# Weight sums behind the transforms: twelve of eighteen sums move to the end of the transform stage, in buffers of the next stage

## The chip, the cores and the metric

The kernel runs on one core of a Trainium2 chip. The core has five engines with an instruction stream each: PE (TensorE, matmuls), DVE (VectorE), ACT (ScalarE), POOL (GpSimd) and SP (SyncE, which only issues DMAs here). An engine takes its instructions one after the other; an instruction can carry waits on semaphores that others raise. The metric is the device time of one execution in microseconds (us), as a median over runs. Lower is better.

## The reference

Eight sequences of 3008 positions and 256 channels go through a real FFT over the positions, a complex 256x256 mix with a soft threshold, and the inverse FFT. Each of the 24064 resulting rows then goes through a gated feed-forward layer with 1536 features.

```python
X = np.fft.rfft(x, axis=1)
Yr = Xr @ w_r - Xi @ w_i + b_r
Yi = Xr @ w_i + Xi @ w_r + b_i
Yr = np.sign(Yr) * np.maximum(np.abs(Yr) - lam, 0.0)   # Yi likewise
y = np.fft.irfft(Y, n=x.shape[1], axis=1)
...
gate = 1.0 / (1.0 + np.exp(-(x @ w_gate)))
val = x @ w_val
return (gate * val @ w_out).astype(np.float32)
```

## The kernel before

**Two halves.** In the first half the transforms are interleaved with a plain feed-forward over the first 9 chunks of 512 rows (`NPL = 9`). Each chunk has 12 feature blocks (`NF = 12`), so there are 108 units, numbered j (chunk c = j // 12, block f = j % 12). A unit is `ffn1` (12 matmuls into the PSUM banks pg and pv, a sigmoid on ACT at L583, a product on DVE at L585, a rounding hh on ACT at L593 and its rest hl on DVE at L594) and `ffn2` (6 matmuls into po, two units later). Between the units stand the steps of the transforms, and after the last forward step the inverse steps `inv_a` of the last two sequences: each takes a tile vf that SP loads (L501), multiplies it on PE (pia, L524), is copied out by ACT (yf, L535) and stored by SP to a DRAM tensor yd (L536). `load_v` is one step ahead of `inv_a`, and there are two vf tiles. In the second half the other rows go through the layer in pairs of chunks, in a form of a Winograd product with 7 instead of 8 block products. That needs sums of weight blocks (`make_t` for the first layer, into the DRAM tensor td; `make_s` for the second, into sd) and sums of input blocks (`first_operands` for the first pair).

**The weight sums.** They are POOL work alone. A `make_t` is 10 arithmetic instructions and a store (L706 to L716); a `make_s` is 13 and two stores (L726 to L742). The feature blocks form six pairs, so there are 12 `make_t` (two for each pair of blocks) and 6 `make_s`. The list `sums` holds them in this order, and the loop over the units takes one every third unit from j = 34 on, so the last comes at j = 85. Their tiles are tb and sa (ring `st`), tt (ring `ry`) and tr, sw and sr (ring `big`) of the transforms' pool p2 and of p3.

**The second half's buffers.** When the forward transforms are done (after j = 88 at the latest) the pool p2 is closed and p4 opened on the same memory. p4 holds nine tiles xop0 to xop8 for rounded operands (each a rounded half and a rest), four tiles w1s0 to w1s3 for first-layer weights, and a tile ypair. The helper `xop` hands out the nine in turn. Three go to `spare`; then the operands of the first pair take, in the order of `first_operands`, a11 xop3, s2 xop4, a12 xop5, s1 xop6, s3 xop7, a22 xop8.

```python
def xop(name):
    count[0] += 1
    return p4.tile([P, 2, HW], F32R, tag=f"xop{(count[0] - 1) % NCB}", bufs=1, name=name)
```

`first_operands` makes the first pair's operands in the last chunk: POOL forms s1 = a21 + a22 (L778, into s1f), s2 = s1 - a11 (L779, into s2f), s3 (L783, in ypair) and s4 (L787); for each operand ACT casts the rounded half (L774) and DVE subtracts the rest (L775). SP loads w1s0 to w1s2 for it (L757), and, placed by the planner of the second half into the same queue, one load of second-layer sums (w2s, L1342), the second pair's rows (ypair, L1198) and the fourth weight tile (w1s3, L1187).

**What sets the order.** In this part of the program a scheduler orders each engine's instructions when the kernel is built; the row order on each engine is then fixed. From the second half's first product on, the kernel's own planner (`arrange`) sets it.

Of the kernel before, what the change touches and what calls it, by code (L numbers as in the profile page):

```python
# [9 lines left out]
F32 = mybir.dt.float32  # L10
F32R = mybir.dt.float32r
# [19 lines left out]
NF2K, NR2K, NLD, NST, NBIG, NMF, NME, NVF, NVO, NHH, NSG, NYF, NYT = 5, 4, 3, 3, 5, 3, 2, 2, 1, 3, 2, 3, 3  # L31
# [10 lines left out]
EARLY = 4  # L42
AT_FIRST = 3
NCONV = 7


def _r12(v):
# [193 lines left out]
def tile_fft_mix_ffn(ctx: ExitStack, tc, x, w_r, w_i, b_r, b_i, w_one, w_out, mf, mi, mis, fa, ft, out):  # L241
    nc = tc.nc

    B, D, S = x.shape[0], w_r.shape[0], R1 * R2
    P = 128
    XR = x.shape[2]
    CT = D // P
    NF = w_one.shape[0]
# [54 lines left out]
    def big(name):  # L303
        return p2.tile([P, 4, D], F32, tag="big", bufs=NBIG, name=name)
# [238 lines left out]
    def result(name):  # L543
        return p3.tile([P, CW], F32, tag="ry", bufs=NYF, name=name)
# [152 lines left out]

    def make_t(fp, i):  # L700
        f0, f1 = 2 * fp, 2 * fp + 1
        g = nc.gpsimd
        b = p2.tile([P, 2, D], F32, tag="st", bufs=NST, name="tb").rearrange("p a (b n) -> p a b n", b=2)
        t = result("tt").rearrange("p (a b n) -> p a b n", a=2, b=2)
        for k, f in enumerate((f0, f1)):
            g.tensor_add(b[:, k], w1h[:, f, i], w1l[:, f, i])  # L706
        t = t.rearrange("p a b n -> p (a b) n")
        g.tensor_sub(t[:, 0], b[:, 1, 0], b[:, 0, 0])
        g.tensor_sub(t[:, 2], b[:, 1, 1], b[:, 1, 0])
        g.tensor_add(t[:, 1], t[:, 2], b[:, 0, 0])  # L710
        g.tensor_sub(t[:, 3], b[:, 0, 1], t[:, 1])
        r = p2.tile([P, 4, 2, P], F32R, tag="big", bufs=NBIG, name="tr")
        for k in (0, 2):
            g.tensor_copy(r[:, k:k + 2, 0], t[:, k:k + 2])
            g.tensor_sub(r[:, k:k + 2, 1], t[:, k:k + 2], r[:, k:k + 2, 0])
        g.dma_start(td[fp, i][:, 3:], r.bitcast(F32))  # L716
        for v, w in enumerate((w1h, w1l)):
            g.dma_start(td[fp, i][:, 0:2, v], w[:, f0, i].bitcast(F32))
            g.dma_start(td[fp, i][:, 2, v], w[:, f1, i, 1].bitcast(F32))

    def make_s(fp):
        g = nc.gpsimd
        if fp >= NH - FG:
            g.dma_start(pd[fp - NH + FG], w2[:, 2 * fp:2 * fp + 2].bitcast(F32))
        a = p2.tile([P, 2, D], F32, tag="st", bufs=NST, name="sa")
        g.tensor_add(a, w2[:, 2 * fp:2 * fp + 2, 0], w2[:, 2 * fp:2 * fp + 2, 1])  # L726
        a11, a21, a12, a22 = a[:, 0, :P], a[:, 0, P:], a[:, 1, :P], a[:, 1, P:]
        w = big("sw").rearrange("p a n -> p (a n)").rearrange("p (k n) -> p k n", n=P)
        zero = w[:, 7]
        g.memset(zero, 0.0)  # L730
        g.tensor_copy(w[:, 0], a11)
        g.tensor_sub(w[:, 1], zero, a12)
        g.tensor_sub(w[:, 3], zero, a22)
        g.tensor_add(w[:, 4], a22, a21)
        g.tensor_sub(w[:, 5], w[:, 4], a11)
        g.tensor_sub(w[:, 6], a11, a21)
        g.tensor_sub(w[:, 2], a12, w[:, 5])
        for k0, k1 in ((0, 4), (4, 7)):
            r = p2.tile([P, 4, 2, P], F32R, tag="big", bufs=NBIG, name="sr")[:, :k1 - k0]
            g.tensor_copy(r[:, :, 0], w[:, k0:k1])  # L740
            g.tensor_sub(r[:, :, 1], w[:, k0:k1], r[:, :, 0])
            g.dma_start(sd[fp // FG, k0:k1, :, fp % FG].rearrange("k p v n -> p k v n"), r.bitcast(F32))  # L742
# [307 lines left out]
    for j in range(NF, len(ffn)):  # L1050
        c, f = divmod(j, NF)
        ffn[j]()
        acc += rates[j >= part]
        if sums and j > 3 * NF - 3 and j % 3 == 1:
            sums.pop(0)()
        while side and (acc >= side[0][0] or j >= (part if len(side) > n_last else end) - 1):
            if len(side) == n_last and j < part:
# [435 lines left out]
```

## Time and profile before

| | us |
|---|---|
| median of 3 runs (lowest to highest) | 2704.79 (2703.63 to 2707.28) |
| the profiled execution | 2710.75 |
| its span, first to last instruction | 2708.9 |
| PE busy | 2662.7 |
| DVE busy | 2140.7 |
| ACT busy | 1670.5 |
| POOL busy | 1055.0 |

The profiled execution is one run of its own, 6.0 us above the median. Busy times are of that execution. A PE instruction's end is modelled, so a busy PE is not PE at its peak.

### The profile page before, as it was taken

The numbers are of one execution on the slowest core, as the hardware profiler recorded it, in microseconds if no ns is written. First come the engines' busy times: TensorE is split into PE (matmuls) and PEld (weight loads), VectorE is DVE, ScalarE is ACT, GpSimd is POOL, SyncE is SP. The second block draws the span as 40 slices with busy tenths as digits, with TensorE's granted clock in tenths as the row PEclk, the third lists the DMA queues.
The fourth block names the chain that finished last, engine by engine and source line by source line (L and its number), as shares of the span: only waits on it lengthen the run. The fifth ranks groups of instructions, "written<-read, shape, count | busy, mean of one in ns | idle before, by whom it ended". The sixth has DMA issues, their size and how long they took to land.

```text
span 2708.9 us, 45080 instructions
## 1 busy us (share of the span) xinstructions
PE 2662.7 (98%) x16763; PEld 2178.5 (80%) x16763; DVE 2140.7 (79%) x3100; ACT 1670.5 (62%) x2852; POOL 1055.0 (39%) x963
## 2 busy tenths in 40 slices
PE   9999999999999999999999999999999999999999
PEld 6778888888888878878788788878788788887877
DVE  5778888687789537888888888888888788888876
ACT  4565554545444446676677766766667667776665
POOL 1441012132235013544555445444554455544532
PEclk9999999999999999999999999999999999999999
DMA  9987655677666675878877888787877788787874
GB/s 294 293 285 197 193 151 168 204 208 208 179 185 179 171 218 164 251 237 251 263 238 246 251 246 265 236 247 237 256 249 242 234 269 239 244 259 243 259 227 135
DMA packets 257659, 617.82 MB, mean 228 GB/s; under 512 B 26464, under 2 KB 130656, under 8 KB 257440
## 3 DMA queue, kind: packets, MB, share of 16 engines
q1 hardware_dynamic: 222720, 521.29, 58.5%
q0 software_dynamic: 34608, 93.60, 16.2%
q8 instruction: 133, 2.18, 0.3%
q14 instruction: 86, 0.70, 0.1%
q10 hardware_dynamic: 112, 0.04, 0.0%
HBM read 440.50 MB, written 116.13 MB: 205 GB/s over the span
## 4 chain that ended last, share of the span: by engine, by line
PE 62%; DMA 14%; DVE 10%; ACT 6%; POOL 4%; issue 3%; SPq 0%; DVEq 0%; POOLq 0%; ACTq 0%
PE z L1155 15%; PE l2z L1155 13%; DMA h<-h 11%; PE c L1155 7%; PE pm L447 4%; PE b L1155 3%; PE pb L413 2%; POOL t L1320 2%; PE pia L524 2%; PE pg L577 2%; ACT op L1331 1%; PE pg L578 1%; POOL h L1320 1%; PE po L605 1%; PE pv L577 1%
## 5 line engine op out<-in xcount | busy, mean ns | idle before, releaser
L1155 PE MATMUL z<-xop,w1s 128*128 128x512 f32 x2592 | 684.3, 391 | 11.4 <-ACT tmp L1246 11.1
L1155 PE MATMUL l2z<-op,w2s 128*128 128x512 f32 x2331 | 599.8, 392 | 3.9 <-DMA w2s<-sd 1.9
L1155 PEld LDWEIGHTS z<-xop,w1s 128*128 128x128 f32 x2592 | 484.9, 188 | 123.8 <-ACT tmp L1246 24.0
L1155 PEld LDWEIGHTS l2z<-op,w2s 128*128 128x128 f32 x2331 | 436.2, 188 | 108.2 <-ACT tmp L1351 7.4
L1246 ACT COPY tmp<-z 128x512 f32<-128x512 f32 x684 | 394.3, 584 | 183.1 <-PE z L1155 175.2
L1333 DVE TENSOR_TENSOR op<-h,op 128x1024 fp32r<-128x1024 f32 (+1 forms) x444 | 472.2, 1078 | 24.9 <-ACT op L1331 19.5
L1331 ACT CAST op<-h 128x1024 fp32r<-128x1024 f32 (+1 forms) x444 | 366.4, 837 | 176.1 <-DMA h<-h 100.1
L1155 PE MATMUL c<-xop,w1s 128*128 128x512 f32 x1296 | 362.1, 392 | 5.1 <-DVE h L1287 3.3
L1293 POOL TENSOR_TENSOR h<-tmp 128x512 f32<-128x512 f32 x114 | 180.1, 1580 | 379.6 <-DVE tmp L1249 362.6
L1155 PEld LDWEIGHTS c<-xop,w1s 128*128 128x128 f32 x1296 | 242.7, 188 | 62.8 <-DVE h L1287 10.5
L1249 DVE TENSOR_TENSOR tmp<-tmp,c 128x512 f32<-128x512 f32 x342 | 231.5, 681 | 62.9 <-ACT tmp L1246 41.2
L1320 POOL TENSOR_TENSOR t<-h 128x512 f32<-128x512 f32 x111 | 173.3, 1562 | 158.0 <-DVE h L1285 158.0
L1265 ACT ACTIVATE tmp<-tmp 128x512 f32<-128x512 f32 x342 | 210.3, 632 | 28.4 <-DVE tmp L1249 28.4
L1314 POOL DMA_DIRECT2D h<-h x148 | 128.3, 900 | 165.8 <-DVE h L1289 56.0
L447 PE MATMUL pm<-w_sb,xsh 128*128 128x256 f32 x1008 | 184.4, 285 | 0.0
L1155 PE MATMUL b<-xop,w1s 128*128 128x512 f32 x648 | 182.3, 390 | 0.0
L447 PEld LDWEIGHTS pm<-w_sb,xsh 128*128 128x128 f32 x1008 | 152.9, 189 | 1.0 <-ACT xsh L429 0.4
L1320 POOL TENSOR_TENSOR h<-h 128x512 f32<-128x512 f32 x111 | 148.9, 1341 | 8.7
L458 ACT CAST yh<-yc 128x512 fp32r<-128x512 f32 x84 | 52.2, 621 | 147.0 <-DVE yc L437 146.9
L1155 PEld LDWEIGHTS b<-xop,w1s 128*128 128x128 f32 x648 | 121.3, 188 | 26.0 <-DVE tmp L1249 0.5
L447 PE MATMUL pm<-w_sb,xsl 128*128 128x256 f32 x504 | 139.6, 277 | 0.0
L585 DVE TENSOR_TENSOR sg<-sg,pv 128x512 f32<-128x512 f32 x108 | 74.1, 686 | 74.2 <-PE pv L579 56.0
(199 smaller groups left out, 4933.0 us busy)
## 6 DMA issues: line engine op xcount, KB each, us to landing
w1s<-td SPq DMA_DIRECT2D x228, 896.0 KB, 6.3
w2s<-sd SPq DMA_DIRECT2D x259, 384.0 KB, 4.3
h<-h POOLq DMA_DIRECT2D x74, 512.0 KB, 6.2
zf<-zd SPq DMA_DIRECT2D x96, 256.0 KB, 3.5
vf<-vd SPq DMA_DIRECT2D x128, 192.0 KB, 4.0
vd<-vz SPq DMA_DIRECT2D x84, 256.0 KB, 2.7
ypair<-yd SPq DMA_DIRECT2D x19, 1024.0 KB, 7.4
out_dram<-acc SPq DMA_DIRECT2D x76, 256.0 KB, 4.3
```

The source lines that it names most:

```text
L447: nc.tensor.matmul(o, l, r, start=(i == 0), stop=(i == len(mms) - 1))
L577: nc.tensor.matmul(t, wh, yth[:, ct], start=(ct == 0), stop=False)
L585: nc.vector.tensor_mul(h, sg, pv)
L1155: nc.tensor.matmul(o, ws[i], vs[j], start=first and not i and not j, stop=i == 1, skip_group_check=not first)
L1246: return t, on("ACT", 0.59, at, lambda: a_.copy(t.get(), z.get()), [z], [t], deps)
L1249: return on("DVE", 0.67, at, lambda: add(t.get(), s.get(), o.get()), [x for x in (s, o) if x is not t], [t], deps)
L1265: return on("ACT", 0.635, at, lambda: a_.activation(t.get(), (o or t).get(), AF.Sigmoid), [o] if o else [], [t], deps)
L1293: made[3, q] = on("POOL", 1.3, 16, lambda: g_.tensor_mul(at_h(3), g22.get(), v.get()), [g22, v], [h], [d22, e22], True)
L1314: return [[on("POOL", 0.9, at + q0, lambda q0=q0, q1=q1: g_.dma_start(h.get()[:, dst, q0:q1], h.get()[:, src, q0:q1], accum_op=ALU.add), [ ...
L1320: return [[on("POOL", 1.3, at + q, lambda q=q: g_.tensor_sub(v()[:, q], h.get()[:, a, q], h.get()[:, b, q]), [h], [o], sum((d[q] for d in ...
L1331: hi = on("ACT", 0.19 + 0.43 * n, at - 8 + q0, lambda q0=q0, q1=q1: a_.copy(t.get()[:, 0, q0:q1], v()[:, q0:q1]), [t_in], [t], sum((d[i] f ...
L1333: lo.append([on("DVE", 0.13 + 0.555 * n, at - 5 + q0, lambda q0=q0, q1=q1: sub(t.get()[:, 1, q0:q1], v()[:, q0:q1], t.get()[:, 0, q0:q1]), ...
```

## The change

The first six `make_t` (the first three pairs of blocks) stay in the first half, now at j = 34, 42, 50, 58, 66 and 74. The other twelve sums (six `make_t`, then six `make_s`) are taken two per unit from the unit after the one in which p4 is opened. They no longer use the rings of p2 and p3: the unrounded values lie in one tile with the tag of w1s3 (`room`), the rounded ones in two tiles with the tags of xop7 and xop8 (`rounded(0)`, `rounded(1)`).

```diff
+LATE = 12
...
+    def room():
+        return p4.tile([P, 14 * P], F32, tag="w1s3", bufs=1, name="sums")
+
+    def rounded(k, n=4):
+        return p4.tile([P, 4, 2, P], F32R, tag=f"xop{7 + k}", bufs=1, name="hilo")[:, :n]
+
     def make_t(fp, i):
...
-        b = p2.tile([P, 2, D], F32, tag="st", bufs=NST, name="tb").rearrange("p a (b n) -> p a b n", b=2)
-        t = result("tt").rearrange("p (a b n) -> p a b n", a=2, b=2)
+        if p4:
+            b, t = (room_[:, 4 * P * k:4 * P * (k + 1)].rearrange("p (a b n) -> p a b n", a=2, b=2)
+                    for room_ in (room(),) for k in range(2))
+        else:
+            b = p2.tile([P, 2, D], F32, tag="st", bufs=NST, name="tb").rearrange("p a (b n) -> p a b n", b=2)
+            t = result("tt").rearrange("p (a b n) -> p a b n", a=2, b=2)
...
-        r = p2.tile([P, 4, 2, P], F32R, tag="big", bufs=NBIG, name="tr")
+        r = rounded(i) if p4 else p2.tile([P, 4, 2, P], F32R, tag="big", bufs=NBIG, name="tr")
...
     def make_s(fp):
...
-        a = p2.tile([P, 2, D], F32, tag="st", bufs=NST, name="sa")
+        v = room()
+        a = v[:, 8 * P:12 * P].rearrange("p (f n) -> p f n", f=2)
...
-        w = big("sw").rearrange("p a n -> p (a n)").rearrange("p (k n) -> p k n", n=P)
+        w = v[:, :8 * P].rearrange("p (k n) -> p k n", n=P)
...
-            r = p2.tile([P, 4, 2, P], F32R, tag="big", bufs=NBIG, name="sr")[:, :k1 - k0]
+            r = rounded(k0 // 4, k1 - k0)
...
-        if sums and j > 3 * NF - 3 and j % 3 == 1:
+        if len(sums) > LATE and j > 3 * NF - 3 and j % 8 == 2:
+            sums.pop(0)()
+        for _ in range(2 if p4 and sums else 0):
             sums.pop(0)()
```

POOL, before, at the end of the first half: the last rows of the sixth `make_s` (L740 to L742), then the sums of the first pair's operands (s1f, s2f, ypair for s3, s2f for s4), then the second pair's first sum.

```order
L740 CAST sr<-sw 128x4x128
L740 CAST sr<-sw 128x3x128
L741 TENSOR_TENSOR sr<-sw,sr 128x4x128
L741 TENSOR_TENSOR sr<-sw,sr 128x3x128
L742 DMA sd<-sr 128x4x256
L742 DMA sd<-sr 128x3x256
L778 TENSOR_TENSOR s1f<-ypair 128x512
L779 TENSOR_TENSOR s2f<-s1f,ypair 128x512
L783 TENSOR_TENSOR ypair<-ypair 128x512
L787 TENSOR_TENSOR s2f<-ypair,s2f 128x512
L1211 TENSOR_TENSOR s1f<-ypair 128x512
```

POOL, in the change, at the same place (L738 to L754 are `make_s`, 12 lines further down than before; L790 is the operand sum of L778, L791 that of L779). These rows are the fifth of the late `make_s`.

```order
L738 TENSOR_TENSOR sums<-w_112 128x512
L742 MEMSET sums 128x128
L743 COPY sums<-sums 128x128
L744 TENSOR_TENSOR sums<-sums 128x128
L745 TENSOR_TENSOR sums<-sums 128x128
L746 TENSOR_TENSOR sums<-sums 128x128
L748 TENSOR_TENSOR sums<-sums 128x128
L747 TENSOR_TENSOR sums<-sums 128x128
L790 TENSOR_TENSOR s1f<-ypair 128x512
L749 TENSOR_TENSOR sums<-sums 128x128
L791 TENSOR_TENSOR s2f<-s1f,ypair 128x512
L752 CAST hilo<-sums 128x4x128
```

The operand sums s1 and s2 now stand in the middle of the fifth late `make_s`, behind the six late `make_t` and four `make_s`; s3 and s4 stand in the same way in the middle of the sixth, and the rest of the sixth is behind them.

ACT, before, in the units j = 96 and 97: the casts of the operands (a is a11 and a12, then s1, s2, s3 and a22), the copies yf of the inverse steps, the sigmoids (L583) and roundings (L593) of the units.

```order
L774 CAST a_12549<-ypair 128x512
L774 CAST a_12697<-ypair 128x512
L774 CAST s_12772<-s1f 128x512
L535 COPY yf<-pia 128x376 x2
L774 CAST s_12624<-s2f 128x512
L583 ACTIVATE sg<-pg 128x512
L774 CAST s_12846<-ypair 128x512
L774 CAST a_12916<-ypair 128x512
L593 CAST hh<-sg 128x512
L535 COPY yf<-pia 128x376 x2
L583 ACTIVATE sg<-pg 128x512
```

ACT, in the change, from the same place on (L786 is the operand cast, L536 the copy yf, L584 the sigmoid, L594 the rounding, L615 the copy of a finished output).

```order
L786 CAST s_12760<-s1f 128x512
L786 CAST s_12612<-s2f 128x512
L594 CAST hh<-sg 128x512
L536 COPY yf<-pia 128x376 x2
L584 ACTIVATE sg<-pg 128x512
L615 COPY ot<-po 128x512
L594 CAST hh<-sg 128x512
L536 COPY yf<-pia 128x376
L584 ACTIVATE sg<-pg 128x512
L786 CAST s_12834<-ypair 128x512
L536 COPY yf<-pia 128x376
L786 CAST a_12904<-ypair 128x512
```

The casts of s1 and s2 moved behind the sigmoid of their unit (j = 96) and stand ahead of its rounding; the cast of s3 moved two units down, between two yf copies of one inverse step, and that of a22 right behind the second of these copies. DVE's subtractions for s1, s2, s3 and a22 moved in the same way: that of s1 stands right ahead of the product of unit 96. The order of PE and SP is the same as before in this part; SP's w2s load, ypair load and w1s3 load stand where they stood, between the yf stores and vf loads of the inverse steps.

## Rows read from the trace of the kernel before

**Rows 1.** The page's first part: each engine's busy time, share of the span and instructions.

```profile
PE 2662.7 (98%) x16763; PEld 2178.5 (80%) x16763; DVE 2140.7 (79%) x3100; ACT 1670.5 (62%) x2852; POOL 1055.0 (39%) x963
```

**Rows 2.** Busy time by stretch (us from the span's start, length, then busy time and instructions of PE, PEld, DVE, ACT and POOL, granted PE clock, DMA share, GB/s). The stretches: transforms before the first sum; the time of the 12 `make_t`; that of the 6 `make_s`; the units behind the forward transforms up to the first pair's operands.

```profile
200.00:350.00 150.00, 148.93 (x1211) 126.67 (x1210) 126.52 (x232) 80.62 (x138) 14.24 (x20) 1.00 0.68 189
376.00:700.00 324.00, 321.59 (x3177) 270.25 (x3176) 259.49 (x433) 166.20 (x296) 79.65 (x121) 0.98 0.65 193
700.00:880.00 180.00, 175.69 (x1975) 156.46 (x1973) 154.85 (x245) 82.96 (x151) 76.34 (x101) 1.00 0.61 180
...
916.00:970.00 54.00, 54.00 (x818) 43.27 (x818) 20.00 (x27) 23.34 (x48) 5.89 (x4) 0.98 0.79 221
```

**Rows 3.** The same columns for the two stretches between 376 and 880 in which the granted PE clock was halved.

```profile
474.30:481.10 6.80, 6.80 (x31) 3.66 (x30) 1.65 (x2) 4.20 (x8) 5.04 (x9) 0.50 0.90 270
556.20:559.60 3.40, 3.40 (x11) 1.67 (x6) 1.93 (x4) 2.06 (x5) 0.00 (x0) 0.51 0.89 282
```

**Rows 4.** One DVE subtraction of the forward transforms (rest of the 128x768 operand), all 84 of them: duration in ns, least, median and most.

```profile
L430 DVE TENSOR_TENSOR xsl<-xsf,xsh x84: 935/958/1401, 191.1 to 896.1; 128x768 fp32r<-128x768 f32 x84
```

**Rows 5.** DVE's timeline at the end of the forward transforms (start, us, what): the last soft threshold.

```profile
912.21 0.69 DVE L437 TENSOR_TENSOR yc<-ys,yc 128x512 f32<-128x512 f32 x1
```

**Rows 6.** POOL's timeline: first and last row of the fastest `make_t`; then the first row, the row before the operand sums' place in the change, the first cast and the stores of the fastest `make_s`; then first row and stores of the slowest `make_s`.

```profile
709.70 1.41 POOL L706 TENSOR_TENSOR tb<-w1h,w1l 128x256 f32<-128x256 f32 x2 [35.52 <-DMA vd<-vz]
...
716.30 0.57 POOL L716 DMA_DIRECT2D td<-tr  x1 [0.15 <-issue]
...
782.81 1.44 POOL L726 TENSOR_TENSOR sa<-w 128x512 f32<-128x512 f32 x1 [15.61 <-DMA vd<-vz]
...
786.90 0.46 POOL L735 TENSOR_TENSOR sw<-sw,sa 128x128 f32<-128x128 f32 x1
787.43 0.53 POOL L737 TENSOR_TENSOR sw<-sa,sw 128x128 f32<-128x128 f32 x1
788.02 1.67 POOL L740 CAST sr<-sw 128x512 fp32r<-128x512 f32 x2
...
792.21 1.54 POOL L742 DMA_DIRECT2D sd<-sr  x2
...
817.81 1.38 POOL L726 TENSOR_TENSOR sa<-w 128x512 f32<-128x512 f32 x1 [23.84 <-DMA vd<-vz]
...
829.26 1.53 POOL L742 DMA_DIRECT2D sd<-sr  x2
```

**Rows 7.** The casts of `make_t` and `make_s` on POOL, all of them: duration in ns, least, median and most.

```profile
L714 POOL CAST tr<-tt x24: 388/400/1131, 381.5 to 713.5; 128x256 fp32r<-128x256 f32 x24
...
L740 POOL CAST sr<-sw x12: 503/704/1232, 722.2 to 873.2; 128x512 fp32r<-128x512 f32 x6, 128x384 fp32r<-128x384 f32 x6
```

**Rows 8.** POOL's timeline at the first pair's operands: the sums s1 and s2 (in brackets the idle time before, and what ended it).

```profile
961.61 1.29 POOL L778 TENSOR_TENSOR s1f<-ypair 128x512 f32<-128x512 f32 x1 [83.06 <-DMA ypair<-yd]
962.98 1.62 POOL L779 TENSOR_TENSOR s2f<-s1f,ypair 128x512 f32<-128x512 f32 x1
```

**Rows 9.** ACT's timeline there: the casts of s1 and s3, the sigmoid of unit 96, and the second yf copy of the inverse step of unit 98.

```profile
962.93 0.62 ACT L774 CAST s<-s1f 128x512 fp32r<-128x512 f32 x1 [0.23 <-POOL s1f L778]
...
965.16 0.59 ACT L583 ACTIVATE sg<-pg 128x512 f32<-128x512 f32 x1
966.32 0.62 ACT L774 CAST s<-ypair 128x512 fp32r<-128x512 f32 x1 [0.57 <-POOL ypair L783]
...
976.48 0.47 ACT L535 COPY yf<-pia 128x376 f32<-128x376 f32 x1 [2.59 <-DMA out_dram<-ot]
```

**Rows 10.** DVE's timeline there: the subtraction for s1, beside POOL's sums, that for s2, and the product of unit 96.

```profile
965.07 1.76 DVE L775 TENSOR_TENSOR s<-s1f,s 128x512 fp32r<-128x512 f32 x1
966.76 0.68 DVE L775 TENSOR_TENSOR s<-s2f,s 128x512 fp32r<-128x512 f32 x1
967.36 0.67 DVE L585 TENSOR_TENSOR sg<-sg,pv 128x512 f32<-128x512 f32 x1
```

**Rows 11.** PE's timeline: three inverse steps (64 small matmuls each).

```profile
970.52 1.15 PE L524 MATMUL pia<-ft_sb,vf 48*64 48x47 f32 x64
...
975.90 1.15 PE L524 MATMUL pia<-ft_sb,vf 48*64 48x47 f32 x64
...
981.28 1.15 PE L524 MATMUL pia<-ft_sb,vf 48*64 48x47 f32 x64
```

**Rows 12.** SP's timeline (it only issues): the w2s load; then a yf store, the second half of a vf load, the ypair load and the vf load behind it.

```profile
965.91 0.42 SPq L1342 DMA_DIRECT2D w2s<-sd  x1
...
976.97 0.37 SPq L536 DMA_DIRECT2D yd<-yf  x1
977.40 0.46 SPq L501 DMA_DIRECT2D vf<-vd  x1
977.95 1.35 SPq L1198 DMA_DIRECT2D ypair<-yd  x1
...
980.42 1.68 SPq L501 DMA_DIRECT2D vf<-vd  x2
```

**Rows 13.** DMA issues: what, queue, count, KB each, median us from issue to landing.

```profile
vf<-vd SPq DMA_DIRECT2D x128, 192.0 KB, 4.0
...
sd<-sr POOLq DMA_DIRECT2D x6, 512.0 KB, 4.0
sd<-sr POOLq DMA_DIRECT2D x6, 384.0 KB, 5.1
```

## The prediction, made before the result was known

> **What bounds the kernel now.** The page's first part comes first: PE is busy for 98% of the span, so only what moves PE counts [rows 1]. The table of stretches says where PE idles: 1.1 of 150 us before any weight sum runs, 2.4 of 324 us beside the twelve `make_t`, 4.3 of 180 us beside the six `make_s`, nothing from 916 to 970 [rows 2]. In two stretches between 376 and 880 the granted clock was 0.50, the lower level of 1.2 GHz, for 6.8 and 3.4 us, which costs half of that, 5.1 us [rows 3]. So whatever the early sums do to PE is inside 6.7 + 5.1 = 11.8 us. The reader is to see next that from 916 on PE has no slack at all, and that DVE (20 of 54 us), ACT (23 of 54) and POOL (5.9 of 54) have plenty [rows 2]. It looks like a good place for POOL work; what decides is not how busy these engines are but what stands behind a waiting row on each.
>
> **What the change takes away early.** All six `make_s` and six of twelve `make_t` leave the stretch from 376 to 880. Beside the `make_s` PE idled 2.4% of the time, before the sums 0.7%, beside the `make_t` 0.7% too [rows 2]. The excess beside the `make_s`, 4.3 - 0.007 x 180 = 3.0 us, is my gain; six `make_t` stay, and for the halved clock I take nothing. Bounds: 0 and 11.8 us.
>
> A DVE row shows how far POOL's sums slow DVE: the 128x768 subtraction takes 935 ns at least, 958 in the median of 84, 1401 at most [rows 4], so most of them are not slowed. The Trainium skill's page "SBUF — State Buffer", section "SBUF: two separate sides", says that VectorE (with two inputs in SBUF) and GpSimd share a port pair that whoever starts first holds for the whole instruction, while the other waits. By that rule each sum taken out frees DVE for its whole length, and the gain would be the full 11.8 us, the forecast 9 us lower; the trace agrees for one row, s1's subtraction beside POOL's sums, 1.76 us against 0.68 [rows 10], but not for the median above.
>
> **When the late sums run.** Their tiles lie on memory of the forward transforms, so POOL cannot start before their last soft threshold ends on DVE, 912.21 + 0.69 = 912.9 us [rows 5]. A `make_t` took 716.30 + 0.57 - 709.70 = 7.17 us at the fastest; a `make_s` 792.21 + 1.54 - 782.81 = 10.94 at the fastest and 829.26 + 1.53 - 817.81 = 12.98 at the slowest [rows 6]. These stood beside a DVE busy for 80 to 86% of the time, the late ones stand beside one busy for 37% [rows 2], so I take the fastest. Lower bound: casts at their least (0.39 us each for `make_t`, 0.50 for `make_s` [rows 7], against 1.47 for two and 1.67 for two in the fastest groups) take 0.7 us off each sum, some 8 us off the whole. Upper bound: halfway to the slowest `make_s`, 9.3% more.
>
> **First wait: s1.** In POOL's new order the operand sum s1 stands behind six `make_t`, four `make_s` and the first eight rows of the fifth (786.90 + 0.46 - 782.81 = 4.55 us [rows 6]): 912.9 + 6 x 7.17 + 4 x 10.94 + 4.55 = 1004.3, and with its own 1.29 us [rows 8] 1005.6. Before, POOL stood idle for 83.06 us ahead of it and made it at 961.61, as soon as ypair had landed [rows 8]. ACT's cast of s1 stands right behind the sigmoid of unit 96, which ended at 965.16 + 0.59 = 965.75 [rows 9]. ACT waits there, and behind it stand unit 96's rounding, the yf copies and all later sigmoids. On DVE the subtraction for s1 stands right ahead of unit 96's product. That product empties the PSUM bank that the next inverse step but one on PE writes: the step of 970.52 [rows 11], in its second matmul. So PE stands at 970.5 until s1 is cast (0.62 [rows 9]), subtracted (1.76, POOL being busy beside it here too) and the product done (0.67 [rows 10]): 1008.6. PE is then 38.1 us late.
>
> **Second wait: s3 and a22.** The operands s3 and a22 lie in xop7 and xop8, the two tiles through which all late sums are rounded. Their casts can't write before the last store of the sixth `make_s` has read these tiles. POOL goes on from 1005.6: one row (0.6) and s2 (1.62 [rows 8]) to 1007.8; the rest of the fifth, 793.75 - 788.02 = 5.7, to 1013.5; the sixth's first eight rows, 4.55, to 1018.1; s3, a row, s4 (1.3 + 0.6 + 1.3) to 1021.3; casts and subtractions, 792.21 - 788.02 = 4.2 [rows 6], to 1025.5. The first store lands 4.0 us behind its issue, at 1029.5, the second is issued 0.8 later and takes 5.1, to 1031.4 [rows 13]. ACT's row for s3 stands ahead of the second yf copy of unit 98's inverse step, so this copy ends at 1029.5 + 0.62 + 0.47 = 1030.6 [rows 9]. SP stores this copy (0.37) before it issues the second half of the next vf load [rows 12], at 1031.0, which lands 4.0 later [rows 13]: 1035.0. The inverse step that needs it began at 981.28 before [rows 11]; with 38.1 us of lateness PE is there at 1019.4 and stands for another 15.6 us. It is now 53.7 us late.
>
> a22's cast and subtraction end at 1031.4 + 0.62 + 0.68 = 1032.7. SP's ypair load for the second pair, which overwrites the tile that a22 is read from, now waits for it: 1032.7 against 977.95 [rows 12], 54.7 us late, and the vf load right behind it likewise. I let this through to PE in full: **54.7 us** (at least 53.7).
>
> **Waits that cost nothing beside these.** SP's w2s load (965.91 before [rows 12]) now waits for the third `make_s`, 912.9 + 43.0 + 21.9 + 9.4 = 987.2, and its store, 991.2; yf stores and vf loads queue behind it, but ACT stands until 1006 anyway. The w1s3 load waits for the last row that reads `room`, 1025.5, and SP comes to it only behind the ypair load at 1032.7. From the second half's first product on the order is the old one, and everything is late by the same amount.
>
> **The clock.** Before, a halved stretch lasted 6.8 or 3.4 us [rows 3], and both followed short stands. Behind the first stand now a halved clock is free, since PE stands again 11 us later; behind the second it costs up to 3.4 us, part of it under the wait for the ypair load's successor. I take 1 us.
>
> **The sum** against the profiled execution, 2710.75 us: + 54.7 + 1 - 3.0 = 2763.5. That execution lay 6.0 us above the median of the runs, so for the median I say 2757 us.
>
> **The rivals.**
>
> *The wait doesn't come, the gain does (faster).* For it: the late stretch has idle DVE, ACT and POOL [rows 2]. The scheduler put s1's cast only one sigmoid later than before, as if s1 were hardly late. It would give 2704.8 - 11.8 = 2693 at best; this is also where the rule on the port pair leads by itself. It decides at 965.75: s1 would have to be there when ACT comes to it. POOL has 53 us until then for 91.4 us of rows in their fastest form, so it would have to be 1.7 times as fast. Chance 0.04.
>
> *Only SP's wait counts.* If the operand sums came early after all, the w2s load would still hold up SP until 991.2; with two stores (0.9) and 4.0 us for a load, the inverse step of 975.90 [rows 11] starts at 996.1, 20 us late. 2704.8 + 20 - 3 = 2722. Chance 0.04.
>
> *The two rounded tiles are too few (slower still).* Between a store and the next write of its tile lie 1.5 us to the sum's end and 5.2 into the next `make_s`, 6.7 us, against 4.0 and 5.1 for a landing in the median [rows 13]. For it: the DMA engines were busy 0.79 from 916 to 970, 0.61 beside the old `make_s` [rows 2]. If landings took 3 us more than there is room for, in nine sums, that is 27 us: 2784. Against it: PE stands, so the other traffic stops. Chance 0.08.
>
> *No effect.* The stand would have to be made up later. PE idles for 46 us in the whole span [rows 1], none of it in one place that could swallow 50. Chance 0.03.
>
> **How the numbers follow.** My forecast, both waits, has 0.81. Low end: 8 us less on POOL and the whole gain, 2710.75 + 46.7 - 11.8 - 6.0 = 2740. High end: 9.3% of the 112.6 us that POOL needs from 912.9 to 1025.5, 10.5 us, 3.4 us of clock, no gain: 2710.75 + 54.7 + 10.5 + 3.4 - 6.0 = 2773. That range leaves out the four rivals and a little of the forecast's own case. A measurement of this kernel can tell 0.2%, 5.4 us, from no change. Slower: 0.81 + 0.08 + 0.04 = 0.93; within: 0.03; faster: 0.04.
>
> **What the changed profile should show.** POOL's first late sum at about 910 to 913 and its last store near 1026, without long idle stretches. s1f (now L790) made near 1005 instead of 961. ACT's longest wait is for s1f, some 40 us, its next for the landing of a store to sd. PE stands twice on the inverse steps, about 38 and 16 us, both in 970 to 1035; the second half's first product comes about 55 us later than before, and all behind it is as it was. Wrong it would be if POOL reached s1 before 966, if the late sums took well under 7 us each, or if PE's stands were filled by rows that I take to be blocked. A first half shorter by more than 5 us would mean that the early gain was undersized.

## The result, and the profile after it

The changed kernel takes 2735.22 us (median of 4 runs, 2733.81 to 2735.96) against 2706.03 (median of 4): 1.0116 times as long, 95% interval 1.0100 to 1.0132. It is slower, as forecast, but by 29 us and not by 52; the time lies 4.8 us below the range. The profiled execution took 2733.81 us, its span 2732.0. Line numbers are 1 to 14 higher than before.

The page's first part (busy time, share, instructions of each engine) answers to [rows 1]; PE idles 77 us where it idled 46:

```profile
PE 2655.3 (97%) x16763; PEld 2173.7 (80%) x16763; DVE 2127.0 (78%) x3100; ACT 1676.7 (61%) x2852; POOL 1034.4 (38%) x963
```

Two of the stretches of [rows 2] (columns as there), and then the 90 us behind them:

```profile
700.00:880.00 180.00, 178.56 (x2016) 161.13 (x2015) 147.48 (x260) 92.67 (x162) 8.23 (x11) 1.00 0.57 162
916.00:970.00 54.00, 39.38 (x620) 31.21 (x612) 12.25 (x14) 13.57 (x28) 51.56 (x88) 0.91 0.77 238
970.00:1060.00 90.00, 64.15 (x717) 51.89 (x718) 24.70 (x31) 26.80 (x51) 35.25 (x49) 0.81 0.50 150
```

The loss is where it was looked for: PE stands for 14.6 of 54 us and 25.9 of 90, and POOL, 5.9 of 54 us busy before, is full (51.6). POOL's timeline shows the first late `make_t`, the first, second, fourth and fifth late `make_s`, s1 and the last stores:

```profile
898.52 1.87 POOL L717 TENSOR_TENSOR sums<-w1h,w1l 128x256 f32<-128x256 f32 x2 [124.40 <-PE pia L525]
...
939.82 1.28 POOL L738 TENSOR_TENSOR sums<-w 128x512 f32<-128x512 f32 x1
...
949.40 1.31 POOL L738 TENSOR_TENSOR sums<-w 128x512 f32<-128x512 f32 x1
...
968.35 1.27 POOL L738 TENSOR_TENSOR sums<-w 128x512 f32<-128x512 f32 x1
...
977.36 1.27 POOL L738 TENSOR_TENSOR sums<-w 128x512 f32<-128x512 f32 x1
...
981.01 1.25 POOL L790 TENSOR_TENSOR s1f<-ypair 128x512 f32<-128x512 f32 x1
...
1000.08 1.53 POOL L754 DMA_DIRECT2D sd<-hilo  x2
```

The waits between 870 and 1070 (engine, line, what ended it; us in total, times, longest), then SP's own:

```profile
PE pia L525 <- DVE sg L586: 27.0, 1, 27.0
ACT s L786 <- POOL s1f L790: 30.9, 1, 30.9
ACT s L786 <- DMA sd<-hilo: 12.7, 1, 12.7
PE pia L525 <- DMA vf<-vd: 6.3, 4, 3.3
PE pia L525 <- ACT yf L536: 5.8, 1, 5.8
...
SPq L1356 <- DMA sd<-hilo: 17.4, 1, 17.4
```

ACT waits 30.9 us for s1 behind the sigmoid of unit 96, PE 27.0 for unit 96's product, ACT another 12.7 for the store of a late sum, SP 17.4 for the third `make_s`: every wait that was forecast, each somewhat shorter. ACT had reached the operands of the first pair when ypair landed, at 949.0 (its casts of a11 and a12):

```profile
948.98 1.14 ACT L786 CAST a<-ypair 128x512 fp32r<-128x512 f32 x2 [1.79 <-DMA ypair<-yd]
```

The waits have a second price. PE stopped at 958.1 with the clock at its full 2.4 GHz and went on at 985.1; from 960.7 to 991.4, and in two later stretches, the granted clock was 0.50, the lower level of 1.2 GHz. Columns as in [rows 2]; first the three stretches, then the time from the sigmoid of unit 88 to that of unit 107 in the change, last the same in the kernel before:

```profile
960.70:991.40 30.70, 6.30 (x72) 5.26 (x73) 7.85 (x7) 5.16 (x10) 30.37 (x49) 0.50 0.39 125
1001.70:1012.00 10.30, 4.08 (x68) 3.55 (x69) 3.36 (x5) 4.46 (x9) 0.00 (x0) 0.50 0.77 228
1018.70:1022.10 3.40, 3.40 (x9) 2.61 (x8) 0.15 (x1) 1.27 (x3) 0.00 (x0) 0.50 0.95 221
902.10:1051.40 149.30, 108.83 (x1495) 87.02 (x1495) 40.74 (x48) 41.62 (x82) 97.06 (x156) 0.85 0.66 201
...
918.10:1020.10 102.00, 101.50 (x1496) 81.60 (x1496) 34.87 (x48) 41.99 (x83) 7.19 (x5) 1.00 0.73 205
```

PE was busy for 13.8 us at the lower level, work that takes half as long at the full clock, so 6.9 us were lost. From the one sigmoid to the other PE stood 40.0 us longer than before (40.5 against 0.5). These two sums make up all but 0.4 of the 47.3 us by which this stretch grew.

**Where it went, unit by unit.** ACT's sigmoid of a unit is a good clock. This table holds, for each profiled execution, its start (under "end": the span) minus that in the kernel before, in us. The last two columns divide 88 to 107: how much longer PE stood there than before, and what the lower clock cost (half of PE's busy time in the stretches in which the granted clock was 0.50). What is left, at most 1.1 us, is longer rows.

| kernel | unit 32 | 56 | 88 | 98 | 107 | end | 56 to 88 | 88 to 107 | PE stood | clock |
|---|---|---|---|---|---|---|---|---|---|---|
| the change | -1.7 | -6.8 | -16.0 | +17.0 | +31.4 | +23.1 | -9.2 | +47.4 | +40.0 | 6.9 |
| other_tiles | +0.2 | -5.1 | -14.4 | +26.7 | +30.4 | +21.9 | -9.3 | +44.8 | +36.9 | 7.6 |
| ops_dve | -0.6 | -5.7 | -15.5 | +8.5 | +14.2 | +10.3 | -9.8 | +29.7 | +22.6 | 6.9 |
| dve_s | +1.3 | -3.9 | -10.3 | +10.9 | +10.1 | +1.3 | -6.4 | +20.4 | +13.4 | 5.9 |
| late_t | -1.6 | -6.6 | -8.0 | -5.4 | -4.9 | -11.4 | -1.4 | +3.1 | +2.7 | 0.0 |
| late_s | +0.7 | -4.1 | -14.0 | -2.3 | -2.7 | -9.6 | -9.9 | +11.3 | +9.1 | 1.8 |
| late_s_ops_dve | +0.5 | -3.0 | -12.9 | -5.7 | -6.6 | -13.1 | -9.9 | +6.3 | +3.0 | 3.0 |
| late_4s | 0.0 | -5.7 | -12.6 | -9.0 | -9.4 | -22.1 | -6.9 | +3.2 | +1.3 | 1.7 |
| fill_only | -0.7 | -5.6 | -16.1 | +2.0 | +0.7 | -0.6 | -10.5 | +16.8 | +10.6 | 6.3 |
| rows_early | +0.6 | -4.2 | -3.2 | +12.9 | +12.4 | +7.0 | +1.0 | +15.6 | +11.2 | 4.1 |
| stores_early | -0.9 | -5.9 | -16.4 | -16.5 | -17.2 | -20.9 | -10.5 | -0.8 | -0.5 | 0.0 |

For the change: 9.2 us won beside the `make_s`, 47.4 lost behind the forward transforms. The rest is a difference between the two executions that were profiled. All kernels gain 3.5 to 5.7 us on that of before from unit 32 to 56, `rows_early` too, whose POOL rows there are the same, and all are faster in the second half, whose own work no edit touches. Two windows show that half, before and changed, from its first copy of a product to the end of the span:

```profile
1028.20:2708.90 1680.70, 1656.20 (x7179) 1343.18 (x7177) 1376.66 (x1815) 1152.99 (x1925) 811.68 (x607) 1.00 0.79 241
```

```profile
1059.50:2732.00 1672.50, 1651.87 (x7180) 1339.64 (x7178) 1381.96 (x1815) 1154.07 (x1925) 809.75 (x608) 1.00 0.79 242
```

The same work took 8.2 us less. With 1.7 us ahead of unit 32 and 5.1 from there to 56 the two executions differ by 15 us outside the stretches of the table's "56 to 88" and "88 to 107". Most of it is granted clock: outside these stretches halved clock cost the execution of before 12.8 us, counted as in the table, and that of the change 1.7. I had taken off 6.0 us for the whole. How much of the 15 us the kernel before has in a usual execution stays open: this one lay 4.7 us above the median of its four runs, and 7 to 8 us above the medians of 2702.35 to 2703.45 that 19 to 23 runs of it have beside the experiments.

### The profile page after: what moved, and what is told of

Its sections match the earlier page's. It is cut to its first block, busy times and chain, and to the rows that moved or that the text cites. A ratio compares the mean times of both kernels' runs of the same rounds, so it can differ in the third digit from the quotient of the medians.

```text
span 2732.0 us, 45068 instructions
## 1 busy us (share of the span) xinstructions
PE 2655.3 (97%) x16763; PEld 2173.7 (80%) x16763; DVE 2127.0 (78%) x3100; ACT 1676.7 (61%) x2852; POOL 1034.4 (38%) x963
## 3 DMA queue, kind: packets, MB, share of 16 engines
q0 software_dynamic: 34608, 93.60, 16.1%
## 4 chain that ended last, share of the span: by engine, by line
PE 66%; DMA 14%; POOL 8%; ACT 5%; DVE 5%; issue 2%; SPq 0%; POOLq 0%; DVEq 0%; ACTq 0%
PE z L1169 14%; PE l2z L1169 13%; DMA h<-h 11%; PE c L1169 7%; PE pm L448 6%; PE b L1169 3%; PE pb L414 3%; POOL t L1334 2%; PE pia L525 2%; PE pg L578 2%; PE po L606 1%; PE pg L579 1%; ACT op L1345 1%; PE pv L578 1%; PE pg L580 1%
## 5 line engine op out<-in xcount | busy, mean ns | idle before, releaser
L1169 PEld LDWEIGHTS c<-xop,w1s 128*128 128x128 f32 x1296 | 241.8, 188 | 62.5 <-DVE h L1301 10.5
L717 POOL TENSOR_TENSOR tb<-w1h,w1l 128x256 f32<-128x256 f32 x12 | 10.8, 915 | 427.8 <-DMA vd<-vz 357.4
```

What stands on the lines that cost most here:

```text
L1169: nc.tensor.matmul(o, ws[i], vs[j], start=first and not i and not j, stop=i == 1, skip_group_check=not first)
```

## The experiments

**How long a late sum is, and where the loss begins: fewer late sums.** Three kernels keep the sums that stay early at their places of before. The numbers count the eighteen sums, twelve `make_t` first; `late_t` has range(6, 12), `late_s` range(12, 18), `late_4s` range(14, 18):

```diff
-LATE = 12
+LATE = range(6, 12)
...
+    early = [(lambda: None) if n in LATE else s for n, s in enumerate(sums)]
+    sums = [sums[n] for n in LATE]
...
```

> Only the six make_t of the last three pairs are late; the other twelve sums stay at their places of before. Theory (the loss is POOL reaching s1 too late, so below a certain length of late work it is nil): six make_t take 41 us from the end of the forward transforms, some 908 us, and are through at about 949, before ypair lands; PE doesn't stand, and only the part of the early gain that belongs to the make_t is left, some 5 us: 2701 us. Rival (late sums cost by themselves, by their transfers or by what they share with DVE): 2710 us or more.

> Only the six make_s are late; the twelve make_t stay at their places of before. Theory: the early gain is that of the make_s, some 9 us. Six make_s of 9.4 us end 57 us behind the end of the forward transforms, and s1 comes some 10 us later than ACT wants it; PE stands for about that, s3 adds little: 2704 to 2708 us. Rival (the second wait, for the rounded tiles, is as long as in the change whatever the amount of work): 2715 us.

> Only the last four make_s are late, all else as before. Theory (the loss begins where POOL's late work passes the landing of ypair): four make_s of 9.4 us end at some 944 us, POOL stands idle before s1, PE doesn't stand for it; of the early gain of 10 us two thirds are left, less 2 us of late loads: 2698 to 2700 us. Rival (a loss that grows with the late work from its first sum on): 2703 us or more.

`late_t`: 2702.65 us, 1.0005 (0.9995 to 1.0014). `late_s`: 2700.40, 0.9985 (0.9972 to 0.9998). `late_4s`: 2697.23, 0.9981 (0.9969 to 0.9993). The first two stand beside a kernel before of 2702.57, the third beside one of 2702.35. POOL's end of the late sums and s1 in `late_t`; ACT's cast of s1 in `late_s`; POOL in `late_4s`:

```profile
946.25 0.57 POOL L727 DMA_DIRECT2D td<-hilo  x1 [0.30 <-POOL hilo L726]
955.54 1.28 POOL L796 TENSOR_TENSOR s1f<-ypair 128x512 f32<-128x512 f32 x1 [8.71 <-DMA ypair<-yd]
```

```profile
961.16 0.62 ACT L792 CAST s<-s1f 128x512 fp32r<-128x512 f32 x1 [9.85 <-POOL s1f L796]
```

```profile
940.55 0.79 POOL L760 DMA_DIRECT2D sd<-hilo  x1 [0.41 <-POOL hilo L759]
952.46 1.29 POOL L796 TENSOR_TENSOR s1f<-ypair 128x512 f32<-128x512 f32 x1 [11.13 <-DMA ypair<-yd]
```

Where POOL is through before ypair lands (8.7 and 11.1 us of idleness ahead of s1), only 3 us are lost behind unit 88; where ACT waits 9.9 us for s1, 11.3; where it waits 31 us, 47.4. The wait begins where the late work passes the landing. `late_4s` has the lowest median of these three. It and `late_s` are faster than the kernel before by 2 to 5 us, with intervals that end just below 1, and can't be told apart. `late_t` came as expected; `late_s` is 4 us and `late_4s` 1 us faster than the lower end of what was. The early gain divides unevenly: -9.9 us (56 to 88) for six `make_s`, -1.4 for six `make_t`.

**The second stand: rounded tiles of their own.**

```diff
-            r = rounded(k0 // 4, k1 - k0)
+            if k0:
+                r = p4.tile([P, FG, 2, P], F32R, tag="w2s2", bufs=1, name="hilo")
+            else:
+                r = pr.tile([P, 4, 2, P], F32R, tag="hilo", bufs=1, name="hilo")
...
```

One of the two is a tile of the second half's weights that is free until then, the other lies in a pool pr that is open for this part of the program only.

> The changed kernel, but the six late make_s round into two tiles of their own, which no operand of the first pair uses. Theory (the operands s3 and a22 wait for the last store of a rounded tile): ACT's 12.7 us wait for a store to sd ahead of the cast of s3 is gone, the long stand of PE for s1, 27 us, stays, and PE's second stand of some 10 us goes: 2725 us. Rival (something else holds at the same place, the room that the w1s3 load needs or SP's queue): PE stands there all the same, 2735 us.

2732.97 us, 1.0112 (1.0097 to 1.0127), beside a kernel before of 2702.57. Not 10 us but 2.6 of the 47.4 went; by the medians it is 2 us, with intervals that overlap. ACT's rows for s1 and s3:

```profile
980.62 0.62 ACT L789 CAST s<-s1f 128x512 fp32r<-128x512 f32 x1 [28.14 <-POOL s1f L793]
...
998.12 0.62 ACT L789 CAST s<-ypair 128x512 fp32r<-128x512 f32 x1 [8.59 <-POOL ypair L798]
```

The wait for a store is gone, but s3's own subtraction stands in the sixth `make_s` on POOL, and ACT waits 8.6 us for that at the same place. The tiles were a second lock on a door that POOL's order kept shut anyway.

**All of POOL's hold taken away: the operand sums on DVE.** To the tiles above:

```diff
-        g = nc.gpsimd
+        g = nc.vector
         ...
         def sums():
             g.tensor_add(s1, a21, a22)
```

> The kernel with rounded tiles of their own, and the four operand sums of the first pair (s1, s2, s3, s4) made by DVE instead of POOL. Theory (all of the late loss runs through POOL's place for s1 to s4, and what SP waits for is a smaller wait behind it): ACT no longer waits for an operand sum, the stand of 25 us for s1 goes; the w2s load on SP still waits for the third late make_s, to about 973, where the trace of the change has it at 970, and the loads of vf queue behind it; PE stands about 15 us for those: 2706 - 10 + 15 + 3 = 2714 us. Rival (the w2s wait costs nothing, as my prediction had it): 2698 us. Rival (ACT or PE waits for something else of POOL's for as long): 2730 us.

2720.53 us, 1.0064 (1.0049 to 1.0078). PE's longest waits and SP's:

```profile
PE po L606 <- DVE ot L615: 16.2, 1, 16.2
PE pia L525 <- DMA vf<-vd: 3.0, 2, 2.7
```

```profile
SPq L1362 <- DMA sd<-hilo: 19.2, 1, 19.2
```

The stand for s1 is gone and another has taken its place: SP holds the w2s load for 19.2 us until the third `make_s` has landed, and yf stores and the store of a finished output queue behind it. ACT waits 15.2 us to write yf, DVE's next copy of an output (ot, L615) begins 2.4 us behind the issue of that store, and PE stands 16.2 us for the copy. The profile doesn't name what DVE waited for; the order fits the held store. So the w2s wait that I priced at nothing beside the others is worth about 16 us by itself. It is nearest to the first theory, 6 us over its 2714. Of the other 13 of the 29.7 us behind unit 88, 6.9 are the lower clock, which the granted clock shows from 967.7 to 988.2, around this stand, and in two stretches of 3.4 us; the rest is in smaller stands, 3.7 us for ACT's hh and some 3 for vf loads.

The same edit with only the six `make_s` late:

> Only the six make_s are late, they round into tiles of their own, and the four operand sums of the first pair are made by DVE. Theory: with only the make_s late ACT waited 9.9 us for s1 and PE stood 8 us for it; this goes, the w2s load's sums are done before SP comes to it, and the early gain of some 10 us is left but for 2 to 3 us of late loads: 2695 to 2698 us, faster than before. Rival (PE stands for the late loads or for DVE's four rows instead): 2704 us.

2698.08 us, 0.9984 (0.9972 to 0.9996): the loss behind unit 88 falls from 11.3 to 6.3 us, half of which is clock. The median lies at the upper end of what was expected, 2.3 us below `late_s`; the intervals overlap.

**DVE as the place for the late `make_s`.** They get another room (w1s2) and other rounded tiles (xop5 and xop6, later those of a12 and s1) than the late `make_t`, and the two kinds of sums take turns:

```diff
+        g, d = nc.vector, nc.gpsimd
...
-            r = rounded(k0 // 4, k1 - k0)
-            g.tensor_copy(r[:, :, 0], w[:, k0:k1])
+            r = rounded(k0 // 4 - 2, k1 - k0)
+            nc.scalar.copy(r[:, :, 0], w[:, k0:k1])
...
-            g.dma_start(sd[fp // FG, k0:k1, :, fp % FG]...
+            d.dma_start(sd[fp // FG, k0:k1, :, fp % FG]...
...
+    sums[6:] = [t for two in zip(sums[12:], sums[6:12]) for t in two]
```

> The changed kernel, but the late make_s are made by DVE with the rounding on ACT, in a room and rounded tiles of their own, one beside each late make_t, which stays on POOL. Theory: POOL is through with six make_t and the issues of the stores at some 948 us, s1 is made when ypair lands, DVE has 34 of 54 us free for some 20 us of rows; no long stand, the early gain of 14 us stays: 2692 us. Rival (DVE's rows stand ahead of the products that PE waits for, 3 us each, six times): 2710 us.

2712.63 us, 1.0047 (1.0029 to 1.0064). Waits of ACT and PE between 900 and 980:

```profile
ACT hilo L753 <- DMA sd<-hilo: 16.2, 6, 7.3
PE pia L525 <- ACT yf L536: 6.3, 1, 6.3
...
PE pia L525 <- DVE sums L747: 0.6, 1, 0.6
```

Neither theory: DVE's rows cost PE 0.6 us of standing, but the rounding, now on ACT, waits for the landing of the tile's last store, 16.2 us in six waits, and ACT's yf copies wait behind it. A wait of POOL, whom nobody needed there, had been moved to an engine that PE needs. The casts of a12 and s1, whose tiles these are, wait another 1.4 and 1.2 us.

**What the sums cost early: rows or stores.** `fill_only` leaves the twelve sums' rows out altogether and stores zeros behind the transforms; `rows_early` makes the rows at their places of before without storing them there; `stores_early` keeps only the stores in the early half, where POOL, with nothing else to do, issues the last of them near 680 instead of 878. The tile of zeros of the first two, and below it the rows that `stores_early` replaces:

```diff
+            filled.append(p4.tile([P, 4, 2, P], F32R, tag="xop8", bufs=1, name="hilo"))
+            nc.gpsimd.memset(filled[0].bitcast(F32), 0.0)
...
-            g.tensor_copy(r[:, :, 0], w[:, k0:k1])
-            g.tensor_sub(r[:, :, 1], w[:, k0:k1], r[:, :, 0])
+            g.memset(r.bitcast(F32), 0.0)
```

> The arithmetic of the twelve sums that the change moves is left out; their stores are issued behind the forward transforms from one tile of zeros. What the change can win early, without what it loses late. Theory (the twelve sums cost the transforms some 14 us, which the trace of the change shows): 2691 us. Rival (my prediction's 3 us; the rest is difference between executions): 2702 us.

> The kernel before, but the twelve sums that the change moves aren't stored where they are made; stores of zeros are issued behind the forward transforms instead, so the sums' transfers leave the transforms and their rows on POOL stay. Theory (POOL's rows slow DVE's rows that read and write SBUF alone, and DVE paces this stretch): as before, 2705 us, and DVE's 128x256 subtraction of the transforms between 700 and 880 takes some 600 ns in the mean as before. Rival (the stores' traffic is what costs): 2692 us.

> The kernel before, but of the twelve sums only the stores are left at their places; the rows on POOL are replaced by one row of zeros for each stored tile. Theory (POOL's rows are what costs): 2692 us, and DVE's 128x256 subtraction between 700 and 880 takes some 430 ns in the mean. Rival (the stores' traffic is what costs): 2705 us.

Beside a kernel before of 2703.45: `fill_only` 2707.30, 1.0008 (0.9994 to 1.0023); `rows_early` 2719.91, 1.0056 (1.0039 to 1.0074); `stores_early` 2690.97, 0.9960 (0.9941 to 0.9979). The two kernels with zeros stored late missed their expectations by 16 and 15 us: the eighteen stores issued in one bunch keep the vf loads from landing. Between 895 and 960 these take 9.2 and 10.6 us to land in the median, against 4.1 in `stores_early`. PE in `fill_only` from 900 to 940:

```profile
PE pia L524 <- DMA vf<-vd: 10.9, 4, 6.7
```

That burden is common to both, so their difference stands: 2719.91 - 2707.30 = 12.6 us for the rows of the twelve sums, and before against `stores_early` gives 2703.45 - 2690.97 = 12.5, each give or take some 5 us. The rows cost. That the early stores cost nothing that shows is read from the table: from unit 56 to 88 `stores_early`, which has them there, and `fill_only`, which has neither rows nor stores there, gain the same 10.5 us. How the rows cost, DVE's rows tell (line, operands, count | busy us, mean ns | idle before). Before, from 700 to 880, and the change, the same units (692 to 864):

```profile
L454 DVE TENSOR_TENSOR ys<-yt 64x256 f32<-64x256 f32 x40 | 21.2, 529 | 0.9
L437 DVE TENSOR_TENSOR yc<-ys,yc 128x512 f32<-128x512 f32 x21 | 17.6, 840 | 0.7
L453 DVE TENSOR_TENSOR ys<-pm,yt 64x256 f32<-64x256 f32 x40 | 16.8, 421 | 2.1
L427 DVE TENSOR_TENSOR xsf<-xsf 128x256 f32<-128x256 f32 x21 | 12.6, 598 | 4.8 <-ACT xsf L425 4.6
L436 DVE TENSOR_SCALAR yc<-ys 128x512 f32<-128x512 f32 x20 | 12.1, 606 | 0.5
```

```profile
L455 DVE TENSOR_TENSOR ys<-yt 64x256 f32<-64x256 f32 x42 | 17.9, 427 | 0.9
L454 DVE TENSOR_TENSOR ys<-pm,yt 64x256 f32<-64x256 f32 x41 | 17.3, 421 | 2.1
L438 DVE TENSOR_TENSOR yc<-ys,yc 128x512 f32<-128x512 f32 x21 | 14.6, 695 | 0.7
L437 DVE TENSOR_SCALAR yc<-ys 128x512 f32<-128x512 f32 x21 | 9.1, 432 | 0.5
L428 DVE TENSOR_TENSOR xsf<-xsf 128x256 f32<-128x256 f32 x21 | 8.9, 424 | 7.5 <-ACT xsf L426 6.9
```

The four rows here that read SBUF alone lose 102, 145, 174 and 174 ns each, 40 x 102 + 21 x 145 + 21 x 174 + 20 x 174 = 14.3 us in a stretch where DVE is busy for 86% of the time; the row with an input in PSUM (pm) takes 421 ns in both. The 128x768 subtraction by which I had judged reads SBUF alone too and lost only 53 ns (1018 against 965). And `rows_early`, then `stores_early`, between 695 and 870:

```profile
L453 DVE TENSOR_TENSOR ys<-pm,yt 64x256 f32<-64x256 f32 x39 | 16.4, 420 | 2.1
L436 DVE TENSOR_SCALAR yc<-ys 128x512 f32<-128x512 f32 x20 | 12.9, 647 | 0.5
L427 DVE TENSOR_TENSOR xsf<-xsf 128x256 f32<-128x256 f32 x21 | 10.9, 519 | 5.2 <-ACT xsf L425 5.0
```

```profile
L453 DVE TENSOR_TENSOR ys<-pm,yt 64x256 f32<-64x256 f32 x42 | 17.7, 421 | 2.2
L427 DVE TENSOR_TENSOR xsf<-xsf 128x256 f32<-128x256 f32 x22 | 9.3, 424 | 8.5 <-ACT xsf L425 7.5
L436 DVE TENSOR_SCALAR yc<-ys 128x512 f32<-128x512 f32 x21 | 8.9, 426 | 0.5
```

It is POOL's arithmetic. In the stretch of `stores_early` POOL runs nothing at all, so these rows show DVE without a neighbour. The timeline of before, from 607 to 880, settles it row by row. This table has the mean length of DVE's rows in ns, and how many, for those during which a row of POOL's arithmetic ran and for all others:

| DVE row | beside POOL | alone |
|---|---|---|
| 128x256, L427 | 820 (10) | 421 (20) |
| 64x256, L454 | 753 (16) | 421 (44) |
| 128x512, one input, L436 | 804 (11) | 427 (19) |
| 128x512, two inputs, L437 | 1100 (8) | 692 (22) |
| 128x768, L430 | 1084 (11) | 957 (19) |
| 64x256, one input in PSUM, L453 | 420 (18) | 421 (42) |

Alone, no row took more than 7 ns over its mean. POOL's rows of zeros in `stores_early` (620 to 678) are another case: the two-input rows beside them keep their length, but two of the three one-input rows that met one took 657 and 912 ns instead of 427:

```profile
656.39 0.97 POOL L738 MEMSET sr<- 128x1024 f32 x1
656.74 0.91 DVE L436 TENSOR_SCALAR yc<-ys 128x512 f32<-128x512 f32 x1
```

That the loss reaches PE through DVE fits the stands of PE between 700 and 897 in before, which end at rows of DVE (2.0 us) and ACT (1.7 us) and none at POOL's or a DMA's; link by link it isn't shown.

## Why the prediction was right in kind and wrong in size

Three terms of the sum were wrong, all in the same direction: the early gain (3.0 us, measured 9.2), the late loss (54.7 us and 1 of clock, measured 47.4) and the step from the profiled execution to the median (6.0 us, 13.7 needed). The first is an error of mechanism, the others of size. With the first two set right the sum gives 2710.75 + 47.4 - 9.2 - 6.0 = 2743.0, which is inside the range: its low end had a gain of 11.8 and a loss of 46.7 in it. It is the third that took the time below the range.

**The early gain, 3.0 us forecast, 9.2 measured.** This step failed in its mechanism. It took PE's idle excess beside the `make_s` for the whole loss. The units themselves came 9.2 us closer together, and 12.5 us is what `stores_early` shows for all twelve sums. PE from unit 56 to 88, before and in the change:

```profile
607.40:918.10 310.70, 303.71 (x3464) 266.91 (x3464) 258.07 (x423) 149.78 (x275) 96.87 (x133) 0.99 0.62 182
```

```profile
600.50:902.10 301.60, 299.04 (x3464) 264.62 (x3464) 241.63 (x423) 154.50 (x275) 24.57 (x39) 1.00 0.58 167
```

Its idle time shrank by 4.4 us, but the same 3464 matmuls also took 4.7 us less. Of these 1.7 are a stretch of halved clock right ahead of unit 88, which before, `late_t` and `rows_early` have and the change hasn't. The other 3.0 are there at full clock in each kernel with the early `make_s`: PE's busy time, taken at full clock, is 301.7 to 302.2 us in these three, 300.4 in `late_4s` with two of the six, and 298.9 to 299.2 in those without. I take it that a matmul waiting for its data at its start is shown as busy; the profile doesn't show it. The time per unit was the thing to read. The second half of the error is [rows 4]: I judged DVE's loss by one row, the 128x768 subtraction, which loses least, and by its median, though most of these rows met no row of POOL. My upper bound, 11.8 us, held by luck. Of the 5.1 us of halved clock in it [rows 3], 3.4 were that execution's own, since `rows_early`, with the same rows, lost 1.7 there, and the hidden 3.0 us were not in it.

The Trainium skill's page "SBUF — State Buffer", section "SBUF: two separate sides", states that VectorE with two inputs in SBUF and a GpSimd instruction that reads SBUF take turns on a port pair, which one of them holds for its whole instruction. The trace agrees that DVE's rows with two inputs in SBUF lose beside POOL's arithmetic (820 against 421 ns), and that those with one in PSUM don't (420 against 421). The one-input row, which lost as well, is outside what I took from that page. That each sum taken out "frees DVE for its whole length" was my overreading: 76 us of POOL's rows cost DVE some 17 us, 14.3 of them in the four rows above.

**When the late sums run.** The start moved to 898.5 instead of 912.9, with the early gain and what the execution of before had lost ahead of it. From there to the end of s1 I had 92.7 us; it took 982.3 - 898.5 = 83.7. The six `make_t` took 6.9 us each (7.17 forecast), the four `make_s` 9.4 (10.94). I had taken the fastest group of before as the price and put the faster casts into the bound; with DVE standing, whole groups are that fast: 9.0 us (968.35 to 977.36) is the same instructions without a neighbour. Together that is 9.0 us less, just past the 8 us of my lower bound.

**The first wait: right.** Same place, same chain (s1's cast, unit 96's product, inverse step), 27.0 us on PE, with some 3 us for vf loads ahead of it; 38.1 were forecast, and the 9.0 us of shorter POOL work account for the difference.

**The second wait: shorter, and only half right in cause.** Forecast were 15.6 us and another 1 for a22; PE stood another 11.6 us (5.8 for the yf copy, 3.3 for one vf load, the rest small). I named the rounded tiles as its cause; `other_tiles` shows that they add 5 us to what POOL's order holds up anyway (1003.57 against 998.12 for s3's cast) and 2.6 to the end.

**The clock: 1 us forecast, 6.9 measured.** I let the halved clock behind the first stand cost nothing, because PE would stand again soon, and I took its length from [rows 3], 6.8 us at most. Behind a stand of 27 us it lasted 30.7, and PE worked 6.3 us of that. The two later stretches add 7.5 us of work at the lower level. So the 47.4 us are 40.0 of standing, where 54.7 were forecast, and 6.9 of clock: the sum came nearer to the forecast than its parts.

**Waits that cost nothing beside these: right, and not to be reused.** SP's wait was hidden in the change. In `ops_dve` it costs 16 us. My rival "only SP's wait counts" had 20 us late and 2722; the kernel that makes it true took 2720.5. That is near by luck: it lost 29.7 us and won 9.8, where the rival had 20 and 3.

**The profiled execution against the median.** I took off 6.0 us. Outside the two stretches that the change alters, the executions of before and of the change differ by 15.1 us, some 11 of them granted clock, and that of the change lay 1.4 us below its median, so 13.7 would have had to come off. The clock of the profiled execution was there to be read, 0.994 in the mean; in most runs of the kernel before beside the experiments it is 0.996 or 0.997, which is worth 5 to 8 us. Together: 2757 - 6.2 for the early gain (9.2 instead of 3.0) - 8.3 for the late loss (47.4 instead of 54.7 + 1) - 7.7 here = 2734.8. The range allowed for the first two errors together, and for nothing in the third.

## What to carry to other kernels

Before work is moved into an idle engine's gap, add up the moved work to the first row that somebody waits for on that engine: here a gap of 50.5 us (898.5 to 949.0, when ypair had landed) stood against 82.5 us of work ahead of s1 (to 981.0), and the excess of 32 us is ACT's wait of 30.9, while four sums that end before ypair lands win 5 us. Add the clock to it: here work at the lower level, during and behind the stands, cost 6.9 us. Price work that is taken off by the time per unit of the loop beside it and by every row of the neighbouring engine, not by PE's idle time. Before a profiled execution is set against a median, look at its granted clock. When a wait is cut, ask what waits next on the same chain: s1, s3 and the w2s load stood one behind another, and each removed wait gave back only the distance to the next.

## What the runs showed of the hardware

- POOL's arithmetic lengthens DVE's rows that read SBUF alone while it runs: 421 to 820 ns (128x256), 421 to 753 (64x256), 427 to 804 and 692 to 1100 (128x512), 957 to 1084 (128x768), in the kernel before. Rows with an input in PSUM keep their length (420 and 421). Over the stretch of the `make_s` the first four lost 21 to 41% in the mean.
- The one-input DVE row (128x512, TENSOR_SCALAR) loses as much as those with two inputs, and it alone loses beside POOL's rows of zeros too: 657 and 912 ns against 427, where two-input rows beside them keep their length (`stores_early`).
- It goes both ways: a `make_s` took 10.94 us at the fastest beside a busy DVE and 9.0 beside one that stood. In `ops_dve` POOL's 128x128 rows took 0.90 us beside DVE's operand rows (952 to 956) and 0.45 while DVE stood (965 to 968).
- Eighteen stores issued one behind another on POOL's queue kept the vf loads from landing: these took 9.2 us in the median (895 to 960, `fill_only`) instead of 4.1, PE stood 10.9 us for them, and some 16 us were lost with the clock. Fifteen of the same stores, issued from 621 to 680 (`stores_early`), cost nothing that shows.
- The granted clock went from 1.00 to 0.50 (1.2 GHz) at 960.7, when PE had stood since 958.1, and was back at 991.4; PE had gone on at 985.1. With two later stretches this cost 6.9 us. In the seven kernels in which PE stood 9 to 40 us longer than before from unit 88 to 107, halved clock cost 1.8 to 7.6 us there.
- The kernel before, 22 times on one chip, spread from 2694.13 to 2711.97 us, so one execution's total settles nothing smaller. The stretches repeat better: from unit 88 to 107 PE's busy time, taken at full clock, is 101.2 to 102.6 us in all twelve profiled executions.
